# Another order in the last softmax over tokens: the Exp table loaded after the last Sin, a product split in two, exponentials copied first, one copy on VectorE

## The chip, the cores and the metric

The kernel runs on one core of one Trainium2 chip. The metric is the device time of one execution in microseconds (us), the median of several runs. TensorE (PE) multiplies matrices, PEld is its weight load; VectorE (DVE), ScalarE (ACT) and GpSimd (POOL) work on tiles; SyncE (SP) issues the transfers.

## The reference

Three layers in a row. The attention is a recurrence over 768 steps for 4 batches and 8 heads; its output is x, 3072 tokens of 384. Then a wide layer and a soft mixture of experts:

```python
h = x @ w_in                       # 3072 x 2048
x = (h * np.cos(h)) @ w_out        # 3072 x 384
logits = x @ phi                   # 3072 x 32 slots
d = np.exp(logits - logits.max(0, keepdims=True))
d /= d.sum(0, keepdims=True) + 1e-09          # softmax over tokens
slot_input = d.T @ x
...                                # per expert: max(slot_input @ w1[e], 0) @ w2[e]
c = np.exp(logits - logits.max(1, keepdims=True))
c /= c.sum(1, keepdims=True) + 1e-09          # softmax over slots
out = c @ slot_out
```

## The kernel before, in words

Tokens come in 12 groups of 256 (group 0 to 11); the 2048 hidden features come in 8 banks of 256, so a bank is one PSUM tile of 128 x 512. The whole order of the work, for all five engines, is written out by hand in the string HEAD: each word is a step, such as `h.11.4.0` (group 11, bank 4, first half), and each step appends its instructions to the queues of its engines. No scheduler changes it. An engine works its queue strictly in that order; where an instruction needs another engine, it waits on a semaphore, and all behind it wait too.

The steps of a bank, with the lines of the profile:

- `h` (L462 to L464, PE): the product x @ w_in into PSUM, in three passes over 3 x 128 rows.
- `turns` (L474, ACT), `rest` (L478, DVE), `cos` (L482, ACT, a Sin), `mul` (L486, DVE): h is reduced by whole turns, its cosine taken, and g = h cos(h) formed.
- `gT` (L494, PE): g is transposed in four pieces into PSUM; `gc` (L499): the transposed tile is copied to SBUF as gt, on ScalarE, or on VectorE for some banks of the last groups. Of the PSUM tiles that gT of the last groups uses there are two, so a gT waits until an earlier gT's tile has been copied out.
- `l` (L507, PE): g times p = w_out @ phi, the logits of the group, summed over all banks (`l.11.5` takes banks 4 and 5, `l.11.7` banks 6 and 7).

When all banks of a group are done, the softmax over tokens takes a step with a running maximum:

- `sum` (L514) copies the logits l to SBUF as lg, `lc` (L520, PE) adds their four parts into PSUM, `max` (L530 to L535, DVE) updates the running maximum and nb, its negative, and `quart` (L541, ACT) copies the logits, cut into four quarters, into the tile dl.
- `exp`: in groups 0 to 10 the exponential is made from a Silu (L556 on ACT, then L563 to L573 on DVE, steps `xt`, `xr`, `xd`). In group 11 it is a true Exp (L551, and L552 for the factor al). Silu, Sin and the copies run from one ScalarE table, Exp needs another one.
- `dT` (L579, PE) transposes exponentials and logits together into one PSUM tile. `dc` (L586, ACT) copies the exponentials out of it as dt, `ltok` (L592, DVE) copies the logits out of it. Both read the same PSUM bank, and the one that stands second in HEAD waits for the first.
- `E` (L603, PE): dt times the eight tiles gt, first half `E.g.0` with gt 0 to 3, second half `E.g.1` with gt 4 to 7. `es` or `esl` (L612, L614, DVE): e_sb = e_sb al + E.

After group 11 the tail is one chain: slot inputs si (L778), expert products (L797, L837), outputs (L868, L870). The softmax over slots of the last tokens uses an Exp too (L627).

The step `tab` (L699, ACT) is an Exp of one column whose result nobody reads; it stands for its table load. Before the change it is in group 9, between `dc.8` and `turns.9.4`. Two weight tiles of 1.5 MB each are loaded after `h.11.4`, and five more after `E.11.1`.

Of the kernel before, what the change touches and what calls it, by code (L numbers as in the profile page):

```python
# [21 lines left out]
def rwkv_moe_kernel(ctx: ExitStack, tc: tile.TileContext, r, k, v, w, u, w_in, w_out, phi, w1, w2, cst, out):  # L22
    nc = tc.nc
# [13 lines left out]
    NBK = MF // 2  # L37
# [6 lines left out]
    ATT = 77  # L44
# [31 lines left out]
    ltok = const.tile([128, NB, 4, SL], F32, name="ltok")  # L76
# [68 lines left out]
    pend = {}  # L145
# [350 lines left out]

    def b_tc(g, i):
        t = gt_p.tile([128, 2, G], F32, tag="gt", name=f"gt{g}_{i}")
        (nc.vector.tensor_copy if NBK * g + i >= ATT and i in (1, 2) else nc.scalar.copy)(t, pend.pop(("gT", g, i)))  # L499
        gt_t[g, i] = t  # L500

    def b_l(g, i):
# [143 lines left out]
    if True:  # L646
# [51 lines left out]
        def exp_table():  # L698
# [6 lines left out]
                "mask": e_mask, "mc": e_mc, "mp": e_mp, "ksn": e_ksn, "bo": e_bo, "bv": e_bv, "U": e_U, "z": e_z, "rz": e_rz, "st": e_st, "y": e_y, "yb": e_yb,  # L705
                "xh": e_xh, "xl": e_xl, "wn": e_wn, "wc": e_wc,
                "h": b_h, "turns": b_turns, "rest": b_rest, "cos": b_cos, "mul": b_mul, "gT": b_t, "gc": b_tc, "l": b_l,
                "sum": s_sum, "lc": s_logits, "max": s_max, "exp": s_exp, "xt": s_exp_t, "xr": s_exp_r, "xd": s_exp_d, "cmb": s_combine, "we": wide, "att": close_attention, "dT": s_dT, "dc": s_dc, "ltok": s_lc,
                "E": s_e_pe, "es": s_e, "close": close_decode}
# [290 lines left out]
lc.8 mul.9.1 h.9.3.0 ks.23 kN.23 h.9.3.1 yb.21 mask.22 ksn.23 U.23 rest.9.0 y.22 cos.9.0 turns.9.3 rz.23.0 mul.9.0 rest.9.3 ru.23  # L1000
l.9.1 bv.22 yb.22 gT.9.0 cos.9.3 max.8 exp.8 st.23.0 mul.9.3 bo.23 xh.22 gc.9.0 z.23.1 st.23.1 xt.8 xr.8 xd.8 h.9.2.0 h.9.2.1
turns.9.2 rT.23 dT.8 h.9.4.0 xl.22 cmb.1.5 zl.23 rest.9.2 sp.23 cos.9.2 gT.9.1 L.23 gc.9.1 h.9.4.1 gT.8.6 h.9.5.0 h.9.5.1 gc.8.6
xh.21 xl.21 dc.8 tab turns.9.4 cmb.0.5 rest.9.4 turns.9.5 h.9.6.0 gT.9.3 h.9.6.1 rest.9.5 cos.9.5 mul.9.2 A.23 ltok.8 E.8.0 E.8.1
l.9.3 cos.9.4 cmb.2.0 mask.23 bv.23 mul.9.5 gc.9.3 cmb.2.1 rz.23.1 y.23 yb.23 turns.9.6 rest.9.6 xh.23 cos.9.6 h.9.7.0 cmb.2.3
mul.9.6 xl.23 gT.9.2 gc.9.2 mul.9.4 h.9.7.1 turns.9.7 rest.9.7 cos.9.7 mul.9.7 cmb.2.2 gT.9.5 gc.9.5 h.10.0.0 gT.9.4 h.10.0.1
l.9.5 l.9.7 gT.9.6 h.10.2.0 turns.10.0 cmb.2.4 rest.10.0 cos.10.0 mul.10.0 sum.9 es.8 h.10.3.0 h.10.3.1 turns.10.3 rest.10.3
# [6 lines left out]
max.10 exp.10 h.11.2.0 mul.11.0 l.11.1 turns.11.6 gT.11.0 gc.11.0 xt.10 rest.11.6 cos.11.6 h.11.2.1 gc.10.5 turns.11.2 mul.11.6  # L1013
rest.11.2 cos.11.2 mul.11.2 h.11.3.0 h.11.3.1 turns.11.3 rest.11.3 cos.11.3 mul.11.3 gT.10.7 h.11.7.0 h.11.7.1 turns.11.7.0
rest.11.7.0 cos.11.7.0 h.11.5.0 h.11.5.1 l.11.3 turns.11.7.1 gc.10.7 rest.11.7.1 cos.11.7.1 mul.11.7.1 xr.10 gT.11.3 turns.11.5
rest.11.5 cos.11.5 gT.11.2 gc.11.2 xd.10 h.11.4.0 h.11.4.1 turns.11.4 dT.10 mul.11.5 ltok.10 gT.11.6 dc.10 E.10.0 E.10.1 gc.11.3
rest.11.4 cos.11.4 mul.11.4 l.11.5 mul.11.7.0 l.11.7 sum.11 we.6 we.10 gT.11.5 lc.11 gc.11.5 gT.11.4 gc.11.6 max.11 quart.11
exp.11 dT.11 ltok.11 gT.11.7 dc.11 gc.11.4 es.10 gc.11.7 we.7 we.8 E.11.0 esl.11.0 we.9 E.11.1 esl.11.1
"""


# [47 lines left out]
```

## Time and profile before

| | |
|---|---|
| median of 3 runs | 549.68 us (548.1 to 550.96) |
| the profiled execution | 549.77 us, of which its span (first to last instruction) 548.0 us |
| mean granted TensorE clock | 0.981 |
| busy in the span | PE 503.2 us, PEld 435.7, DVE 433.4, ACT 315.5, POOL 125.3 |
| chain that ended last | PE 62%, DVE 21%, ACT 8%, DMA 4%, issue 3% |

Matmuls are pipelined, so a row's duration overlaps with the next; what an engine waits for is read from the idle time before a row, given in brackets, and from the distance between starts. A clock of 1.00 is 2.4 GHz, 0.50 is 1.2 GHz. Times in the rows below are counted from the start of the span.

### The profile page before, as it was taken

What the parts mean: (1) busy time and instruction counts of PE and PEld (TensorE: products, weight loads), DVE (VectorE), ACT (ScalarE), POOL (GpSimd) and SP (SyncE); (2) the same over time, 40 slices, a digit from 0 to 9 for tenths busy, and PEclk for the clock granted to TensorE, in tenths of its full rate; (3) what the DMA queues carried; (4) which work ended last, traced back from release to release, by engine and by line L of the source; (5) the groups of instructions that cost most, each with busy time, mean ns of one, the idle gap of its engine ahead of it and who ended that gap; (6) DMA issues with size and microseconds to landing.
All of it is one profiled execution on the core that took longest, in us unless ns stands there. A gap on an engine that the chain in (4) does not pass through costs nothing.

```text
span 548.0 us, 16247 instructions
## 1 busy us (share of the span) xinstructions
PE 503.2 (92%) x6850; PEld 435.7 (80%) x6850; DVE 433.4 (79%) x823; ACT 315.5 (58%) x661; POOL 125.3 (23%) x163
## 2 busy tenths in 40 slices
PE   2777879989999999999999999999999999997994
PEld 1546667879898898998988988999888899883674
DVE  4999898998889879887878898989788867664423
ACT  3256567646757465666555754656557756664422
POOL 4520120254044213321420420533034000000400
PEclk9988999999999999999999999999999999998997
DMA  8994656444432433411440342173031683377949
GB/s 209 268 240 110 157 115 182 123 75 74 74 60 44 76 57 60 74 35 27 75 73 10 66 89 45 22 132 54 16 60 32 232 317 144 112 264 275 403 175 273
DMA packets 146712, 67.52 MB, mean 123 GB/s; under 512 B 127568, under 2 KB 134736, under 8 KB 146640
## 3 DMA queue, kind: packets, MB, share of 16 engines
q1 hardware_dynamic: 146640, 66.49, 47.9%
q8 instruction: 54, 0.88, 0.7%
q14 instruction: 18, 0.15, 0.1%
HBM read 61.75 MB, written 4.72 MB: 121 GB/s over the span
## 4 chain that ended last, share of the span: by engine, by line
PE 62%; DVE 21%; ACT 8%; DMA 4%; issue 3%; SPq 0%; ACTq 0%; DVEq 0%
PE h L462 9%; PE h L464 9%; PE h L463 9%; PE gT L494 6%; PE E L603 4%; PE l L507 3%; DMA rawi<-in_moe_w_in_dram 3%; PE y L288 3%; PE A L208 3%; DVE L L222 2%; PE U L259 2%; DVE g L478 2%; PE hps L797 2%; PE so L837 2%; DVE pt L164 2%
## 5 line engine op out<-in xcount | busy, mean ns | idle before, releaser
L462 PE MATMUL h<-x,wu 128*128 128x256 f32 x573 | 172.0, 300 | 1.3 <-DVE g L486 1.3
L464 PE MATMUL h<-x,wu 128*128 128x256 f32 x573 | 161.4, 282 | 1.2 <-ACT wu L410 1.2
L463 PE MATMUL h<-x,wu 128*128 128x256 f32 x573 | 161.3, 281 | 0.0
L462 PEld LDWEIGHTS h<-x,wu 128*128 128x128 f32 x573 | 109.2, 191 | 3.5 <-DVE g L486 1.7
L464 PEld LDWEIGHTS h<-x,wu 128*128 128x128 f32 x573 | 109.0, 190 | 1.4 <-ACT wu L410 1.4
L463 PEld LDWEIGHTS h<-x,wu 128*128 128x128 f32 x573 | 109.3, 191 | 0.2
L482 ACT ACTIVATE g<-g,half_pi 128x512 f32<-128x512 f32 (+1 forms) x97 | 69.4, 719 | 42.4 <-DVE g L478 41.4
L486 DVE TENSOR_TENSOR g<-g,h 128x512 f32<-128x512 f32 x96 | 64.8, 677 | 28.0 <-ACT g L482 27.5
L474 ACT ACTIVATE g<-h 128x512 int32<-128x512 f32 x96 | 57.0, 596 | 39.8 <-PE h L464 32.9
L478 DVE SCALAR_TENSOR_TENSOR g<-g,h 128x512 f32<-128x512 int32 x96 | 65.0, 678 | 16.8 <-ACT g L474 15.7
L251 POOL TENSOR_TENSOR bv<-vz,bo 64x384 f32<-64x384 f32 x48 | 43.9, 914 | 140.1 <-DVE bo L243 78.1
L499 ACT COPY gt<-gT 128x512 f32<-128x512 f32 x92 | 53.3, 583 | 31.2 <-PE gT L494 30.6
L494 PE MATMUL gT<-cs,g 128*128 128x128 f32 x384 | 58.1, 275 | 0.3 <-ACT gt L499 0.2
L494 PEld LDWEIGHTS gT<-cs,g 128*128 128x128 f32 x384 | 43.7, 140 | 6.2 <-issue 3.3
L169 POOL TENSOR_TENSOR ru<-rn,u_b 128x384 f32<-128x384 f32 x24 | 27.3, 1136 | 58.2 <-issue 19.5
L193 POOL MEMSET L<- 64x512 f32 x32 | 16.7, 521 | 96.1 <-PE y L288 81.5
L156 DVE TENSOR_TENSOR_SCAN qt<-wf,one_b 128x520 f32<-128x520 f32 x24 | 30.5, 1270 | 7.3 <-ACT wf L151 7.2
L222 DVE TENSOR_TENSOR L<-A,cs 64x512 f32<-64x512 f32 x48 | 33.1, 689 | 3.8 <-PE A L208 2.6
L274 ACT COPY rzs<-z 64x192 f32<-64x192 f32 x96 | 33.4, 348 | 3.6 <-DVE z L269 2.6
L187 DVE TENSOR_TENSOR L<-rT,pt 64x512 f32<-64x512 f32 x48 | 32.9, 686 | 1.6 <-PE rT L141 0.6
L164 DVE TENSOR_TENSOR_SCAN pt<-wf,ini_f 128x520 f32<-128x520 f32 x24 | 31.7, 1320 | 0.1
L208 PE MATMUL A<-L,ks 128*64 128x64 f32 (+1 forms) x768 | 28.1, 226 | 2.8 <-DVE ks L199 2.1
(175 smaller groups left out, 836.3 us busy)
## 6 DMA issues: line engine op xcount, KB each, us to landing
we<-in_moe_w_dram SPq DMA_DIRECT2D x16, 1536.0 KB, 10.4
rawi<-in_moe_w_in_dram SPq DMA_DIRECT2D x7, 768.0 KB, 6.0
wn<-in_w_dram SPq DMA_DIRECT2D x24, 192.0 KB, 4.1
kn<-in_k_dram SPq DMA_DIRECT2D x24, 192.0 KB, 3.9
rn<-in_r_dram SPq DMA_DIRECT2D x24, 192.0 KB, 3.9
vz<-in_v_dram SPq DMA_DIRECT2D x48, 96.0 KB, 3.2
rzs<-in_v_dram SPq DMA_DIRECT2D x96, 48.0 KB, 2.8
out_dram<-ob SPq DMA_DIRECT2D x17, 256.0 KB, 3.7
```

The source lines that it names most:

```text
L208: nc.tensor.matmul(ps[64 - 64 * a:128 - 64 * a, s, :], lhsT=ks[k, s, :], rhs=L[k, a, s, :], start=True, stop=True)
L222: nc.vector.tensor_tensor(out=L[h, a], in0=ps[h], in1=mask[h].unsqueeze(1).to_broadcast([64, NS, C]), op=ALU.mult)
L251: nc.gpsimd.tensor_tensor(out=bv[h], in0=vn_t[j][h, :, c, :], in1=bo[h].to_broadcast([64, H, D]), op=ALU.mult)
L462: nc.tensor.matmul(hp, lhsT=wh, rhs=xh[:, c, :], start=(c == 0), stop=False)
L463: nc.tensor.matmul(hp, lhsT=wh, rhs=xl[:, c, :], start=False, stop=False)
L464: nc.tensor.matmul(hp, lhsT=wl, rhs=xh[:, c, :], start=False, stop=(c == KD - 1))
L474: nc.scalar.activation(gt.bitcast(I32), hp, AF.Copy, bias=0.25, scale=1.0 / TWO_PI)
L478: nc.vector.scalar_tensor_tensor(out=gt, in0=gt.bitcast(I32), scalar=-TWO_PI, in1=hp, op0=ALU.mult, op1=ALU.add)
L482: nc.scalar.activation(gt, gt, AF.Sin, bias=half_pi[:, 0:1])
L486: nc.vector.tensor_tensor(out=gt, in0=gt, in1=hp, op=ALU.mult)
L494: nc.tensor.transpose(ps[:, tt, mm, :], gt[:, mm, tt * 128:(tt + 1) * 128], ident)
L499: (nc.vector.tensor_copy if NBK * g + i >= ATT and i in (1, 2) else nc.scalar.copy)(t, pend.pop(("gT", g, i)))
```

## The change

Five things are done, four of them by moving words in HEAD:

1. `tab` leaves group 9 and stands behind `cos.11.4`, the last Sin of the kernel.
2. `rest.11.4` and `cos.11.4` move ahead of the copies that stood before them (`ltok.10` on DVE, `gc.11.3` on ACT); `gc.11.3` now stands behind `tab`.
3. `E.10.1` leaves its place behind `E.10.0` and stands behind `lc.11`; so do `es.10` and `gc.11.5`, later than `max.11`.
4. In groups 10 and 11 `dc` stands ahead of `ltok`.
5. `gc` of bank 5 runs on VectorE in groups 9, 10 and 11, where it ran on ScalarE.

```diff
-        (nc.vector.tensor_copy if NBK * g + i >= ATT and i in (1, 2) else nc.scalar.copy)(t, pend.pop(("gT", g, i)))
+        (nc.vector.tensor_copy if NBK * g + i >= ATT and i in (1, 2, 5) else nc.scalar.copy)(t, pend.pop(("gT", g, i)))
...
-xh.21 xl.21 dc.8 tab turns.9.4 cmb.0.5 rest.9.4 turns.9.5 h.9.6.0 gT.9.3 h.9.6.1 rest.9.5 cos.9.5 mul.9.2 A.23 ltok.8 E.8.0 E.8.1
+xh.21 xl.21 dc.8 turns.9.4 cmb.0.5 rest.9.4 turns.9.5 h.9.6.0 gT.9.3 h.9.6.1 rest.9.5 cos.9.5 mul.9.2 A.23 ltok.8 E.8.0 E.8.1
...
-rest.11.5 cos.11.5 gT.11.2 gc.11.2 xd.10 h.11.4.0 h.11.4.1 turns.11.4 dT.10 mul.11.5 ltok.10 gT.11.6 dc.10 E.10.0 E.10.1 gc.11.3
-rest.11.4 cos.11.4 mul.11.4 l.11.5 mul.11.7.0 l.11.7 sum.11 we.6 we.10 gT.11.5 lc.11 gc.11.5 gT.11.4 gc.11.6 max.11 quart.11
-exp.11 dT.11 ltok.11 gT.11.7 dc.11 gc.11.4 es.10 gc.11.7 we.7 we.8 E.11.0 esl.11.0 we.9 E.11.1 esl.11.1
+rest.11.5 cos.11.5 gT.11.2 gc.11.2 xd.10 h.11.4.0 h.11.4.1 turns.11.4 dT.10 mul.11.5 rest.11.4 gT.11.6 dc.10 cos.11.4 tab ltok.10
+E.10.0 mul.11.4 l.11.5 mul.11.7.0 l.11.7 sum.11 gc.11.3 gT.11.5 gc.11.6 lc.11 we.6 we.10 E.10.1 max.11 quart.11 exp.11 gc.11.5
+gT.11.4 es.10 dT.11 gT.11.7 dc.11 ltok.11 gc.11.4 gc.11.7 we.7 we.8 E.11.0 esl.11.0 we.9 E.11.1 esl.11.1
```

ScalarE's queue in the last group, before, from dc.10 to dc.11 (gt_3 is the copy gc.11.3, g_4 the cosine cos.11.4, dl the quarters and then the exponentials, dt the copied exponentials):

```order
L586 COPY dt_7319<-dT_7309 64x64 x2
L499 COPY gt_3_7339<-gT_3_7270 128x512
L482 ACTIVATE g_4_7307<-g_4_7307,half_pi 128x512
L499 COPY gt_5_7366<-gT_5_7359 128x512
L499 COPY gt_6_7373<-gT_6_7314 128x512
L541 COPY dl_112<-lc_7364 32x64 x4
L551 ACT_TABLE_LOAD
L551 ACTIVATE dl_112,sg_7385<-dl_112,nb_7378 128x64
L552 ACTIVATE al_7384<-dl_112,nb_7378 128x1
L586 COPY dt_7397<-dT_7388 64x64 x2
```

The same piece of ScalarE's queue in the changed kernel:

```order
L586 COPY dt_7317<-dT_7308 64x64 x2
L482 ACTIVATE g_4_7306<-g_4_7306,half_pi 128x512
L699 ACT_TABLE_LOAD
L699 ACTIVATE half_pi<-half_pi 128x1
L499 COPY gt_3_7345<-gT_3_7269 128x512
L499 COPY gt_6_7352<-gT_6_7312 128x512
L541 COPY dl_112<-lc_7354 32x64 x4
L551 ACTIVATE dl_112,sg_7378<-dl_112,nb_7371 128x64
L552 ACTIVATE al_7377<-dl_112,nb_7371 128x1
L586 COPY dt_7397<-dT_7390 64x64 x2
```

The table load moved from just before the Exp to just behind the last Sin; gc.11.3 went behind it, and gc.11.5 left the queue.

TensorE's queue in the same place, before, from the last product of group 10 to the transpose of the exponentials:

```order
L603 MATMUL E_7322<-gt_7_7264,dt_7319 32x256
L507 MATMUL l_7152<-g_4_7307,p_sb 32x256 x2
L507 MATMUL l_7152<-g_5_7275,p_sb 32x256 x2
L507 MATMUL l_7152<-g_6_7157,p_sb 32x256 x2
L507 MATMUL l_7152<-g_7_7236,p_sb 32x256 x2
L494 MATMUL gT_5_7359<-cs,g_5_7275 128x128 x4
L520 MATMUL lc_7364<-lg_7353,cs 128x256
L494 MATMUL gT_4_7368<-cs,g_4_7307 128x128 x4
L579 MATMUL dT_7388<-cs,dl_112 128x128
```

And in the changed kernel, from the last product of E.10.0 to the first of E.10.1:

```order
L603 MATMUL E_7324<-gt_3_6988,dt_7317 32x256
L507 MATMUL l_7151<-g_4_7306,p_sb 32x256 x2
L507 MATMUL l_7151<-g_5_7274,p_sb 32x256 x2
L507 MATMUL l_7151<-g_6_7156,p_sb 32x256 x2
L507 MATMUL l_7151<-g_7_7235,p_sb 32x256 x2
L494 MATMUL gT_5_7347<-cs,g_5_7274 128x128 x4
L520 MATMUL lc_7354<-lg_7343,cs 128x256
L603 MATMUL E_7324<-gt_4_7057,dt_7317 32x256
```

The eight products of E.10.1 moved behind lc.11; the transposes gT.11.4 and dT.11 follow them.

VectorE's queue before, from mul.11.5 to lg (the copy of `sum`):

```order
L486 TENSOR_TENSOR g_5_7275<-g_5_7275,h_5_7240 128x512
L592 COPY ltok<-dT_7309 64x2x32 x2
L478 SCALAR_TENSOR_TENSOR g_4_7307<-g_4_7307,h_4_7288 128x512
L486 TENSOR_TENSOR g_4_7307<-g_4_7307,h_4_7288 128x512
L486 TENSOR_TENSOR g_7_7236<-g_7_7236,h_7_7216 128x256
L514 COPY lg_7353<-l_7152 128x256
```

And in the changed kernel:

```order
L486 TENSOR_TENSOR g_5_7274<-g_5_7274,h_5_7239 128x512
L478 SCALAR_TENSOR_TENSOR g_4_7306<-g_4_7306,h_4_7287 128x512
L592 COPY ltok<-dT_7308 64x2x32 x2
L486 TENSOR_TENSOR g_4_7306<-g_4_7306,h_4_7287 128x512
L486 TENSOR_TENSOR g_7_7235<-g_7_7235,h_7_7215 128x256
L514 COPY lg_7343<-l_7151 128x256
```

rest.11.4 changed places with ltok.10.

## Rows read from the trace of the kernel before

**Rows 1.** Timeline of TensorE, last group: start us, us, engine, line, operation [idle before].
```profile
490.14 0.27 PE L579 MATMUL dT<-cs,dl 128*128 128x128 f32 x1
...
491.67 1.93 PE L603 MATMUL E<-gt,dt 128*32 128x256 f32 x32 [0.82 <-ACT dt L586]
493.63 1.07 PE L507 MATMUL l<-g,p_sb 128*32 128x256 f32 x16
494.63 0.66 PE L494 MATMUL gT<-cs,g 128*128 128x128 f32 x4
495.24 0.70 PE L520 MATMUL lc<-lg,cs 128*128 128x256 f32 x2
...
499.10 0.33 PE L579 MATMUL dT<-cs,dl 128*128 128x128 f32 x1 [2.48 <-ACT dl L551]
...
500.49 3.33 PE L603 MATMUL E<-gt,dt 128*32 128x256 f32 x32 [0.63 <-ACT dt L586]
...
504.94 2.81 PE L778 MATMUL si<-wo_sb,et 128*32 128x256 f32 x64
```

**Rows 2.** Timeline of ScalarE in the same stretch.
```profile
490.34 0.60 ACT L474 ACTIVATE g<-h 128x512 int32<-128x512 f32 x1 [0.43 <-PE h L464]
491.20 0.42 ACT L586 COPY dt<-dT 64x64 f32<-64x64 f32 x2 [0.26 <-DVE ltok L592]
491.65 0.59 ACT L499 COPY gt<-gT 128x512 f32<-128x512 f32 x1
492.13 0.72 ACT L482 ACTIVATE g<-g,half_pi 128x512 f32<-128x512 f32 x1
...
496.44 0.85 ACT L541 COPY dl<-lc 32x64 f32<-32x64 f32 x4
497.31 1.28 ACT L551 ACT_TABLE_LOAD   x1
498.60 0.35 ACT L551 ACTIVATE dl<-dl,nb 128x64 f32<-128x64 f32 x1
...
500.02 0.42 ACT L586 COPY dt<-dT 64x64 f32<-64x64 f32 x2 [0.79 <-DVE ltok L592]
```

**Rows 3.** Timeline of VectorE in the same stretch.
```profile
491.14 0.69 DVE L478 SCALAR_TENSOR_TENSOR g<-g,h 128x512 f32<-128x512 int32 x1
492.88 1.02 DVE L486 TENSOR_TENSOR g<-g,h 128x512 f32<-128x512 f32 x2 [1.05 <-ACT g L482]
494.76 0.42 DVE L514 COPY lg<-l 128x256 f32<-128x256 f32 x1 [0.86 <-PE l L507]
495.98 0.42 DVE L530 TENSOR_REDUCE mx<-lc 128x1 f32<-128x256 f32 x1 [0.79 <-PE lc L520]
...
499.46 0.47 DVE L592 COPY ltok<-dT 64x64 f32<-64x64 f32 x2 [2.67 <-PE dT L579]
```

**Rows 4.** Windows: stretch, length, busy PE, PEld, DVE, ACT, POOL, granted clock, DMA, GB/s.
```profile
500.00:502.00 2.00, 1.51 (x16) 0.80 (x20) 0.84 (x2) 1.48 (x4) 0.82 (x1) 0.50 0.03 11
```

**Rows 5.** Timeline of ScalarE and of TensorE's weight load around the old tab, group 9.
```profile
430.53 1.28 ACT L699 ACT_TABLE_LOAD   x1
431.82 0.20 ACT L699 ACTIVATE half_pi<-half_pi 128x1 f32<-128x1 f32 x1
...
438.18 0.64 PEld L288 LDWEIGHTS y<-L,rzs 128*32 128x32 f32 x32 [0.46 <-ACT rzs L274]
```

**Rows 6.** All waits of TensorE from 425 to 492 us: total us, times, longest.
```profile
PE E L603 <- ACT dt L586: 0.8, 1, 0.8
PE y L288 <- ACT rzs L274: 0.3, 1, 0.3
```

**Rows 7.** Timeline of VectorE where the copies of bank 5 come in, groups 9 to 11.
```profile
450.55 0.69 DVE L478 SCALAR_TENSOR_TENSOR g<-g,h 128x512 f32<-128x512 int32 x1 [0.84 <-ACT g L474]
...
475.19 0.68 DVE L499 COPY gt<-gT 128x512 f32<-128x512 f32 x1
...
480.29 0.69 DVE L486 TENSOR_TENSOR g<-g,h 128x512 f32<-128x512 f32 x1 [1.49 <-ACT g L482]
```

## The prediction

> **What bounds the kernel now.** I read the page first: TensorE has most of the chain that ended last, so before asking what an edit saves I ask whether TensorE waits there. The list of its waits answers that for the whole stretch from group 9 to the end of h.11.4: two entries in 67 us, one of 0.3 us and one of 0.8 [rows 6]. So up to dT.10 (490.14) TensorE is the bound, and work taken from ScalarE there gains only what TensorE stood waiting for. From 490.14 on it is different. The three timelines of the last group [rows 1 to 3], read together from row to row, show one dependent chain through three engines with TensorE mostly idle: turns.11.4 490.34, rest 491.14, cos 492.13, mul 492.88, l 493.63, the copy lg 494.76, lc 495.24, max 495.98, quart 496.44, table load 497.31, Exp 498.60, dT.11 499.10, ltok 499.46, dc.11 500.02, E.11 500.49, which ends at 503.82. All that follows hangs on that end: the slot inputs start behind it [rows 1], and the five late weight loads are issued after it, so they shift with it. Last the windows: at 500 to 502 the granted clock is 0.50, 1.2 GHz [rows 4]. E.11 takes 3.33 us for the 32 rows that took E.10 1.93 [rows 1]. What TensorE did before the fall was to wait 2.48 us for the Exp, and then only transposes [rows 1].
>
> **The change part by part.** All sums are against the profiled execution, 549.77 us, 0.09 above the median of the runs shown.
>
> *The old tab.* It removes three table loads from ScalarE, for its own Exp and for the Sin and the Silu that had to load back (one of the three stands in the rows), and a 0.20 us activation: 3 x 1.28 + 0.20 = 4.04 us of ScalarE [rows 5]. TensorE saw of it only its wait for the last copy rz.23, 0.46 us by the weight load's row [rows 5], 0.3 by the list of waits [rows 6]. The ends are 0 and 0.46. I take 0.46, since behind it TensorE has no other wait up to E.10, and E.10's wait lies behind h.11.4.
>
> *The copies of bank 5 on VectorE.* Each is 0.68 us there [rows 7] and leaves ScalarE 0.59 us [rows 2]. In group 9 the copy goes ahead of work that a little later leaves VectorE idle for 0.84 us; in group 10 it falls into an idle 1.49 us [rows 7]. Both are covered, though the first with little to spare; uncovered, each could cost up to 0.68. In group 11 it stands behind max.11, where VectorE had nothing to do until ltok at 499.46, idle 2.67 us [rows 3]; only gT.11.7 waits for it. I take 0 for all three. es.10 goes into the same idle time.
>
> *rest and cos forward.* turns.11.4 ends at 490.94 [rows 2]; rest can start at 490.98 instead of 491.14. It ends 0.69 later, 491.67. cos, which no longer waits for gc.11.3, starts at 491.70 instead of 492.13: 0.43 saved. mul and l follow at the old distances, 492.45 and 493.20 [rows 1, 3], and lg at 494.33. dc.10 no longer waits for ltok.10 [rows 2], so it follows turns.11.4 at about 490.85 and E.10.0 starts near 491.3; half of E.10's 1.93 is done by 492.3, before l needs TensorE.
>
> *The new place of tab, and a wait that it adds.* cos ends at 492.42; load 1.28, activation 0.20, gc.11.3 0.59: the copy ends at 494.49. gT.11.5 needs the PSUM tile that this copy frees, and lc stands behind gT.11.5 on TensorE. So gT.11.5 starts at about 494.52, only 0.11 before its old 494.63 [rows 1]. If lc keeps its old distance of 0.61 to it, 0.11 is saved; if lc hangs on lg alone, as before, 0.43. I take 0.3, as the old 0.61 was set by lg (494.76 + 0.42), not by the transposes: lc at 494.94.
>
> *Exp without its load.* quart starts 1.20 behind lc in the old trace, when max (495.98 + 0.42) and ScalarE's two copies end together [rows 2, 3]. max alone gives the same distance: quart at 496.14. The Exp comes 0.87 behind it, where the load started: 497.01 against 498.60, 1.59 saved; dT.11 at 497.51.
>
> *dc ahead of ltok.* dc.11 starts 0.92 behind dT.11 now, because ltok reads the bank first; ltok starts 0.36 behind it [rows 1 to 3]. With places changed dc.11 starts at 497.87 and E.11 0.47 later, 498.34, against 500.49: 2.15 saved. E.11.1 needs gc.11.4 and gc.11.7, which stay behind dc on ScalarE: 2 x 0.59 from 498.29, ready by 499.5. Its product with gt 7 comes at about 499.5, so I count nothing for it, at most 0.2.
>
> *E.11 at full clock.* Between lc and dT.11 TensorE now has E.10.1 (half of 1.93) and gT.11.4, so the wait of 2.48 shrinks to below 0.7. I take the clock to stay at 2.4 GHz. E.11 then takes 1.93 instead of 3.33 [rows 1], 1.40 saved. The ends for this term are 0 and 1.40.
>
> Sum: 0.46 + 2.15 + 1.40 = 4.0 us off. 549.77 - 4.0 = **545.8 us**.
>
> The load's price is where rule and rows part. In the trace the load takes 1.28 us, starts 0.02 after the last quarter copy and is followed by the Exp within 0.01 [rows 2]; the load of group 9 likewise is followed at once [rows 5]. The Trainium skill, "ScalarE: Activation LUTs", section "What ACT_TABLE_LOAD costs", gives about 1283 ns for the load and about 1380 ns more for a drain, 2.66 us for each switch. By that figure gc.11.3 would end 1.38 us later, and by an estimate from it the sum would be about 2.6 us instead of 4.0. The rows show the 1283 ns and no drain, so I go by them.
>
> **The rivals.**
>
> *A. The clock still falls before E.11.* For it: E.10.0 leaves a new gap before l (E.10.0 ends near 492.3, l starts at 493.20), and from E.10.1 to E.11 there are again transposes only, about 2 us. Against it: the gap of 0.82 before E.10 left E.10 at 1.93 [rows 1], and the long idle is gone. E.11 keeps its 3.33: 549.77 - 0.46 - 2.15 = 547.2.
>
> *B. The early gain is lost on VectorE.* For it: gc.9.5 stands in VectorE's queue ahead of a rest and a mul whose PSUM tile a later h needs, and the idle time behind it is only 0.84 [rows 7]. If it delays TensorE by its 0.68 and the 0.46 don't arrive: 549.77 - 4.0 + 0.46 + 0.68 = 546.9.
>
> *C. The load holds gc.11.3 longer.* If a switch behind a running Sin costs one load's length more, 1.28, then gT.11.5, lc and all behind come 1.28 later: 547.1. Against it: each load in the rows runs on without a gap. The drain of that page of the Trainium skill is such a mechanism, with nearly this price.
>
> *D. Slower.* The mechanism is the same clock at another place: it falls in the new gap before l.11.5 and stays at 1.2 GHz until the slot inputs are done. By E.11's ratio 3.33/1.93 = 1.73 [rows 1], l gains 0.78, lc 0.5, E.11 1.40 over the forecast and si 2.05: 4.7 in all, against 4.0 saved, so 550.5, and more if it lasts into the expert products. It decides from about 8 us at the low clock on. Against it: the mean granted clock of the whole span is 0.981, and TensorE has more to do in this stretch than before, not less.
>
> That the change doesn't do what it says I exclude: the queues show one load left behind the first, and none before the Exp.
>
> **How the numbers follow.** Forecast 0.66, A 0.16, B 0.11, C 0.04, D 0.03. 0.5% is 2.75 us, about what a measurement of this kernel can tell from no change; it puts the border at 546.9. The forecast lies 1.1 below it and A, C just above; B is on it. Faster: 0.61 of the forecast, half of B and 0.05 of A: 0.72. Slower by more than 0.5%: 0.02 of D. The rest, 0.26, is within. The range: down to 544.7, with the runs of before spread over 2.86 us and lc at its better end; up to 547.6, which takes in A, B and C with a little for that spread.
>
> **What would show it.** In the changed profile: one table load besides the first, right behind the last Sin; no wait of y for rz.23; gT.11.5 waiting for gc.11.3; Exp within 0.1 us of quart's end; dc.11 about 0.36 behind dT.11 and ltok behind it; E.11 starting about 2.6 earlier and lasting about 1.9 at clock 1.00; the stretch from E.11's end to the end of the span unchanged. I am wrong if E.11 still shows 0.50, if a PE wait on a rest or mul appears in groups 9 to 11, or if the tail behind E.11 lengthens, for instance because a weight load comes late.

## The result

| | before | changed |
|---|---|---|
| median of 5 runs each | 549.68 us (548.1 to 550.96) | 544.25 us (542.96 to 545.2) |
| ratio | | 0.9909, 95% interval 0.9886 to 0.9931 |
| the profiled execution | 549.77 us, span 548.0 | 544.25 us, span 542.5 |
| mean granted clock | 0.981 | 0.98 |

The changed kernel is faster by 0.9%. It lies on the side that was forecast, but 1.55 us below the forecast of 545.8 and 0.45 below the low end of the range, 544.7.

### The profile after

The timeline of TensorE in the changed kernel, last group (start us, us, engine, line, operation, idle before it), which answers to [rows 1]:

```profile
488.02 0.27 PE L579 MATMUL dT<-cs,dl 128*128 128x128 f32 x1
488.13 0.60 PE L494 MATMUL gT<-cs,g 128*128 128x128 f32 x4
490.18 1.07 PE L603 MATMUL E<-gt,dt 128*32 128x256 f32 x16 [1.46 <-DVE ltok L592]
491.06 1.07 PE L507 MATMUL l<-g,p_sb 128*32 128x256 f32 x16
492.33 0.66 PE L494 MATMUL gT<-cs,g 128*128 128x128 f32 x4 [0.20 <-ACT gt L499]
492.82 0.60 PE L520 MATMUL lc<-lg,cs 128*128 128x256 f32 x2
493.35 1.07 PE L603 MATMUL E<-gt,dt 128*32 128x256 f32 x16
494.35 0.66 PE L494 MATMUL gT<-cs,g 128*128 128x128 f32 x4
495.30 0.33 PE L579 MATMUL dT<-cs,dl 128*128 128x128 f32 x1 [0.28 <-ACT dl L551]
495.46 0.60 PE L494 MATMUL gT<-cs,g 128*128 128x128 f32 x4
496.13 2.15 PE L603 MATMUL E<-gt,dt 128*32 128x256 f32 x32
...
499.38 2.81 PE L778 MATMUL si<-wo_sb,et 128*32 128x256 f32 x64
```

The wait of 2.48 us ahead of dT.11 has become 0.28, and E.11 takes 2.15 us instead of 3.33. There is a wait that nobody forecast, 1.46 us ahead of E.10.0.

ScalarE in the same stretch, which answers to [rows 2]:

```profile
488.71 0.41 ACT L586 COPY dt<-dT 64x64 f32<-64x64 f32 x2
489.57 0.72 ACT L482 ACTIVATE g<-g,half_pi 128x512 f32<-128x512 f32 x1 [0.45 <-DVE g L478]
490.31 1.28 ACT L699 ACT_TABLE_LOAD   x1
491.60 0.20 ACT L699 ACTIVATE half_pi<-half_pi 128x1 f32<-128x1 f32 x1
491.71 1.06 ACT L499 COPY gt<-gT 128x512 f32<-128x512 f32 x2
493.92 0.85 ACT L541 COPY dl<-lc 32x64 f32<-32x64 f32 x4 [1.15 <-DVE mx L530]
494.80 0.35 ACT L551 ACTIVATE dl<-dl,nb 128x64 f32<-128x64 f32 x1
...
495.66 0.42 ACT L586 COPY dt<-dT 64x64 f32<-64x64 f32 x2 [0.23 <-PE dT L579]
496.11 1.07 ACT L499 COPY gt<-gT 128x512 f32<-128x512 f32 x2
```

The load now stands right behind the last Sin, and the Exp follows the quarter copies at once. The copies between them run without a further load. dc.11 waits for dT.11 alone.

VectorE there, which answers to [rows 3], and ahead of it the copy of bank 5 in group 9, which answers to the first of [rows 7]:

```profile
443.65 0.68 DVE L499 COPY gt<-gT 128x512 f32<-128x512 f32 x1
...
448.42 0.69 DVE L478 SCALAR_TENSOR_TENSOR g<-g,h 128x512 f32<-128x512 int32 x1 [0.24 <-ACT g L474]
...
488.85 0.69 DVE L478 SCALAR_TENSOR_TENSOR g<-g,h 128x512 f32<-128x512 int32 x1 [0.34 <-ACT g L474]
489.57 0.47 DVE L592 COPY ltok<-dT 64x64 f32<-64x64 f32 x2
490.32 1.02 DVE L486 TENSOR_TENSOR g<-g,h 128x512 f32<-128x512 f32 x2 [0.29 <-ACT g L482]
492.20 0.42 DVE L514 COPY lg<-l 128x256 f32<-128x256 f32 x1 [0.86 <-PE l L507]
493.46 0.42 DVE L530 TENSOR_REDUCE mx<-lc 128x1 f32<-128x256 f32 x1 [0.83 <-PE lc L520]
```

The copy of group 9 was taken out of idle time, 0.84 us before and 0.24 now; in group 10 the 1.49 us of [rows 7] became 0.88.

The granted clock over E.11 in the windows (columns as in [rows 4], which had 0.50 there), and y of group 9 on TensorE, which was broken by the wait of [rows 5] and is now one run of 64 products; TensorE waits nowhere from 425 to 487 us, where [rows 6] had two waits up to 492:

```profile
496.00:498.00 2.00, 1.93 (x33) 1.04 (x32) 1.07 (x4) 1.16 (x3) 0.82 (x1) 1.00 0.90 350
```
```profile
433.60 1.93 PE L603 MATMUL E<-gt,dt 128*32 128x256 f32 x32
435.79 1.08 PE L288 MATMUL y<-L,rzs 128*32 128x64 f32 x64
436.79 0.55 PE L297 MATMUL y<-cs,bv 128*128 128x128 f32 x3
```

### The profile page after: what moved, and what is told of

Same layout as the page of the kernel before. It is cut to its first block, busy times and chain, and to the rows that moved or that the text cites. A ratio compares the mean times of both kernels' runs of the same rounds, so it can differ in the third digit from the quotient of the medians.

```text
span 542.5 us, 16245 instructions
## 1 busy us (share of the span) xinstructions
PE 502.9 (93%) x6850; PEld 436.4 (80%) x6850; DVE 435.2 (80%) x826; ACT 310.7 (57%) x655; POOL 125.4 (23%) x163
## 4 chain that ended last, share of the span: by engine, by line
PE 67%; DVE 18%; ACT 5%; DMA 4%; issue 2%; SPq 2%; DVEq 0%; ACTq 0%
PE h L462 10%; PE h L464 10%; PE h L463 10%; PE gT L494 6%; PE l L507 4%; PE E L603 3%; PE A L208 3%; PE y L288 3%; PE U L259 2%; DMA vz<-in_v_dram 2%; PE hps L797 2%; DMA rawi<-in_moe_w_in_dram 2%; PE so L837 2%; DVE L L222 2%; DVE pt L164 2%
## 5 line engine op out<-in xcount | busy, mean ns | idle before, releaser
L499 ACT COPY gt<-gT 128x512 f32<-128x512 f32 x89 | 51.6, 584 | 28.7 <-PE gT L494 28.1
L156 DVE TENSOR_TENSOR_SCAN qt<-wf,one_b 128x520 f32<-128x520 f32 x24 | 30.6, 1275 | 7.3 <-ACT wf L151 7.3
```

The source lines that it names most:

```text
L499: (nc.vector.tensor_copy if NBK * g + i >= ATT and i in (1, 2, 5) else nc.scalar.copy)(t, pend.pop(("gT", g, i)))
```

## Where the 5.5 us between the two profiles lie

The two spans differ by 5.5 us, but 1.3 of it is there before anything that the change touches. My marker is a scan of the attention on VectorE (L156), on code that is the same in both kernels. It is the 23rd of 24 such scans in either kernel; the expectations below call it the last, which it is not. It starts at these times, first in the kernel before, then in the changed one:

```profile
394.20 1.24 DVE L156 TENSOR_TENSOR_SCAN qt<-wf,one_b 128x520 f32<-128x520 f32 x1
```
```profile
392.87 1.24 DVE L156 TENSOR_TENSOR_SCAN qt<-wf,one_b 128x520 f32<-128x520 f32 x1
```

So I cut each profile into three: the **head** up to the start of this scan, the **middle** from there to the start of si, which holds all of the change, and the **tail** from si to the end of the span. Head, middle and tail are 394.20, 110.74 and 43.06 us before, and 392.87, 106.51 and 43.12 after. The middle lost 4.23 us.

Theory T: the change is worth what the middle shows, and the head scatters from execution to execution. Rival R: the changed kernel has a shorter head each time. Inside the middle most parts of the change were tested for their own price; the cosine's new place ahead of gc.11.3 was not undone by itself. The diffs below show only the words of HEAD that move. Each expectation counts from the start of the scan either to the end of the span or, in the last three, to the start of si; both readings stand in the table. I go by the start of si, because the tails turned out to scatter too, from 42.88 to 43.26 us.

| run | head | middle | middle against the changed kernel | scan to end of span | TensorE's wait at dT.11 | length of E.11 |
|---|---|---|---|---|---|---|
| before | 394.20 | 110.74 | +4.23 | 153.80 | 2.48 | 3.33 |
| e1, before again | 392.16 | 110.70 | +4.19 | 153.74 | 2.48 | 3.30 |
| e2 | 391.60 | 109.61 | +3.10 | 152.6 | 2.48 | 2.72 |
| changed | 392.87 | 106.51 | 0 | 149.63 | 0.28 | 2.15 |
| e8, changed again | 394.14 | 106.50 | -0.01 | 149.76 | 0.28 | 2.15 |
| e3 | 392.96 | 107.79 | +1.28 | 150.94 | 1.56 | 2.15 |
| e4 | 392.64 | 107.38 | +0.87 | 150.26 | 1.44 | 2.15 |
| e5 | 390.87 | 107.13 | +0.62 | 150.03 | 0.28 | 2.15 |
| e6 | 391.28 | 106.83 | +0.32 | 149.82 | 0.28 | 1.93 |
| e7 | 393.07 | 106.42 | -0.09 | 149.63 | none | 1.93 |
| e9 | 392.46 | 106.30 | -0.21 | 149.24 | 0.28 | 1.93 |
| e11 | 390.39 | 109.68 | +3.17 | 152.81 | 2.71 | 2.71 |
| e12 | 392.72 | 106.70 | +0.19 | 149.68 | 0.28 | 2.15 |

Two profiles of one kernel agree in the middle to 0.04 us, while heads lie anywhere from 390.39 to 394.20. The scans of L156 show where the heads part: in the 13 traces the first of them, at about 6 us, starts within 0.8 us, the seventh, at about 115 us, within 3.5, and the marker within 3.8. So nearly all of the scatter arises in the first 115 us.

## The experiments

### Is the head a matter of the kernel? (e1, e8)

Both kernels were run again without an edit.

> The kernel before, unchanged, so that its first 394 us are seen a second time. Theory T: those 394 us are the same code in both kernels and their length scatters from execution to execution by 1 to 2 us, so the start of the last scan over tokens (L156) can fall anywhere from 392 to 395 us here, while the stretch from that start to the end of the span stays at 153.8 us within 0.3. Rival R: the kernel before reaches that scan late each time, at 394.2 us within 0.3, and the changed one early, at 392.9.

> The changed kernel, unchanged, so that its first 393 us are seen a second time. Theory T: from the start of the last scan to the end 149.63 us within 0.3, while that start itself may fall anywhere from 392 to 395 us. Rival R: it falls at 392.9 us within 0.3 again.

Measured: 547.82 us (545.49 to 549.32) for the kernel before, 544.22 (542.53 to 545.65) for the changed one. The heads changed places: 392.16 before, 394.14 after. R falls, and T stands, though its 392 was too high: four other heads lie between 390.39 and 391.60. The marker in the two repeats, that of the kernel before first:

```profile
392.16 1.24 DVE L156 TENSOR_TENSOR_SCAN qt<-wf,one_b 128x520 f32<-128x520 f32 x1
```
```profile
394.14 1.24 DVE L156 TENSOR_TENSOR_SCAN qt<-wf,one_b 128x520 f32<-128x520 f32 x1
```

Over all 68 runs of the kernel before, on several chips, the median is 548.52 us and the mean 548.38 (545.04 to 551.14); 10 of them are at 549.68 or above. The 11 runs of the changed kernel have a mean of 544.14. The means differ by 4.24 us, the middle by 4.2.

### The old table load alone (e2)

```diff
-dc.8 tab turns.9.4
+dc.8 turns.9.4
```

> The kernel before with one edit: the table load ahead of group 9's turns is taken out, so that the load comes back ahead of the last Exp, as before. Measured from the start of the last scan to the end of the span. Theory T: the 0.78 us that the changed kernel had gained at E.8 and y of group 9 is due to this load alone, so 153.1 us (153.80 less 0.7 to 0.8), and the engine time of y is one unbroken run of 64. Rival: the 0.78 us comes from another order of the queues and the load is worth the 0.46 us of its own wait at most, 153.3 to 153.4.

Measured: 547.29 us, ratio to the kernel before 0.9973 (0.9956 to 0.999); the middle 1.1 us shorter. To the end it takes 152.6, which is 0.5 below T. From the scan to dT.10 it takes 95.22 us, against 95.94 before and 95.15 in the changed kernel: 0.72 of the 0.79 us is this load, nearly as T has it, and more than the 0.46 of the rival. In the kernel before y of group 9 begins, breaks and goes on like this:

```profile
437.23 0.65 PE L288 MATMUL y<-L,rzs 128*32 128x64 f32 x32
438.19 0.80 PE L288 MATMUL y<-L,rzs 128*32 128x64 f32 x32 [0.30 <-ACT rzs L274]
438.92 0.55 PE L297 MATMUL y<-cs,bv 128*128 128x128 f32 x3
```

From the first product to the next line's it is 1.69 us here and 1.00 in the unbroken row of the changed kernel: the break costs 0.69, more than either wait that is named for it. The remaining 0.4 us of e2 are not the load: after the same 2.48 us of waiting the granted clock was low already under dT.11 and came back earlier in E.11. E.11 started 1.54 us behind dT.11, where it had been 1.39 in the kernel before, but took 2.72 us and not 3.33:

```profile
495.78 0.48 PE L579 MATMUL dT<-cs,dl 128*128 128x128 f32 x1 [2.48 <-ACT dl L551]
...
497.32 2.72 PE L603 MATMUL E<-gt,dt 128*32 128x256 f32 x32 [0.21 <-ACT dt L586]
```

### Parts of the new order undone (e3 to e6)

e3, no early load:

```diff
-cos.11.4 tab ltok.10
+cos.11.4 ltok.10
```

> The changed kernel without its early table load: everything else of its order stays, and the load falls ahead of the last Exp again (1.28 us on ScalarE). Measured from the start of the last scan to the end, the changed kernel has 149.63 us. Theory T: the Exp comes 1.28 us later less the little that ScalarE waited ahead of it, so TensorE waits at dT.11 for 1.3 to 1.4 us where it waited 0.28, the clock stays at 2.4 GHz over E.11 since the wait is shorter than the 2.48 us of before, and the stretch is 150.7 us. Rival, the clock: the wait is enough for the granted clock to fall over E.11, which then takes 3.3 us as before, and the stretch is 152.0 to 152.2 us.

Measured: 545.73 us, ratio 0.9945 (0.9927 to 0.9963). The load is back ahead of the Exp, and TensorE waits at dT.11 for exactly its length more, 1.56 against 0.28:

```profile
494.87 1.28 ACT L551 ACT_TABLE_LOAD   x1
496.17 0.35 ACT L551 ACTIVATE dl<-dl,nb 128x64 f32<-128x64 f32 x1
```
```profile
496.66 0.33 PE L579 MATMUL dT<-cs,dl 128*128 128x128 f32 x1 [1.56 <-ACT dl L551]
...
497.50 2.15 PE L603 MATMUL E<-gt,dt 128*32 128x256 f32 x32
```

The clock stayed at 1.00, so T holds and its rival falls: the load by itself is worth 1.28 us.

e4, E.10 in one piece:

```diff
-E.10.0 mul.11.4 l.11.5
+E.10.0 E.10.1 mul.11.4 l.11.5
...
-we.10 E.10.1 max.11
+we.10 max.11
```

> The changed kernel with the second half of E of group 10 put back behind the first. Theory T: the 16 products (1.07 us) then stand ahead of l.11.5, lg and lc, and the max, Exp and dT.11 come 0.9 to 1.0 us later, TensorE waits at dT.11 for 1.2 to 1.3 us more than now; from the start of the last scan to the end 150.6 us against 149.63. Rival, the clock: the longer wait at dT.11 lets the granted clock fall, E.11 takes 3.3 us, and the stretch is 152 us. Rival, no matter: the split is hidden, because the softmax waits for its scores (mul, lg) on VectorE and not for TensorE, and the stretch is 149.6 us.

Measured: 544.76 us, ratio 0.9924 (0.9907 to 0.9941), middle +0.87. The split is not hidden; T's price was nearly right, and the clock held through a wait of 1.44 us:

```profile
490.04 1.93 PE L603 MATMUL E<-gt,dt 128*32 128x256 f32 x32 [1.46 <-DVE ltok L592]
...
493.37 0.70 PE L520 MATMUL lc<-lg,cs 128*128 128x256 f32 x2
...
495.94 0.33 PE L579 MATMUL dT<-cs,dl 128*128 128x128 f32 x1 [1.44 <-ACT dl L551]
```

The 0.87 is a price within the new order. E.10 starts 2.17 us behind dT.10 here and started 1.53 behind it in the kernel before; lc comes 5.50 behind dT.10 and came 5.10. So the split in part only makes good the later start of E.10 that the other moves bring.

e5, the copies of dT.11 in the old order:

```diff
-gT.11.7 dc.11 ltok.11
+gT.11.7 ltok.11 dc.11
```

> The changed kernel with the copies of dT.11 in the old order: VectorE's transposed turns (ltok) ahead of ScalarE's copy of the exponentials (dc). Both read the one bank that dT.11 fills. Theory T: ScalarE's copy waits for VectorE's, as it did before (0.79 us ahead of dc.11 in rows of the kernel before, 0.23 in the changed one), E.11 starts 0.5 to 0.6 us later, and the stretch from the start of the last scan to the end is 150.2 us against 149.63. Rival: the two engines read the bank side by side and the order is worth nothing, 149.6 us.

Measured: 544.1 us, ratio 0.9917 (0.9895 to 0.9938), middle +0.62. ScalarE's copy waits 0.81 us for VectorE's, against 0.23 in the changed kernel, and E.11 behind it:

```profile
494.28 0.42 ACT L586 COPY dt<-dT 64x64 f32<-64x64 f32 x2 [0.81 <-DVE ltok L592]
```
```profile
494.75 2.15 PE L603 MATMUL E<-gt,dt 128*32 128x256 f32 x32 [0.66 <-ACT dt L586]
```

e6, bank 5 back on ScalarE:

```diff
-i in (1, 2, 5) else
+i in (1, 2) else
```

> The changed kernel with the copies of bank 5 (gc.9.5, gc.10.5, gc.11.5) back on ScalarE. Theory T: those of groups 9 and 10 cost nothing on either engine, since TensorE waits for neither; gc.11.5 now stands between the last Exp and dc.11 on ScalarE and takes about 0.6 us there, of which TensorE's transposes hide a part, so E.11 starts about 0.3 us later: 149.9 us against 149.63 from the start of the last scan. Rival: the copies on VectorE had held up its own turns in groups 9 and 10, and taking them back gains there what is lost in group 11: 149.6 us or less.

Measured: 543.84 us, ratio 0.9919 (0.9897 to 0.9941), middle +0.32. From the scan to dT.10 it is 95.14 us, with the copies on VectorE 95.15: in groups 9 and 10 the move costs and gains nothing. All of the 0.32 arises in group 11, where gc.11.5 stands between the Exp and dc.11, and gT.11.7 waits for it:

```profile
494.48 0.66 PE L494 MATMUL gT<-cs,g 128*128 128x128 f32 x4 [0.47 <-ACT gt L499]
```

The runs' medians could not have told these last prices from nothing: e6 is 0.3 us longer in its middle and has a lower median than the changed kernel. The cut profile does. The prices of e2 to e6 (0.72, 1.28, 0.87, 0.62, 0.32) need not add up to the 4.23 of the middle: each was measured beside the other parts, and the clock's share, below, is in none of them.

### Does the clock depend on that wait? (e11)

e3 and e4 together.

> The changed kernel with two parts undone at once: no early table load (e3) and the second half of E of group 10 back behind the first (e4). Each alone cost 1.28 and 0.87 us from the start of the last scan to the start of si and left the granted clock at 1.00. Theory T: the wait of TensorE ahead of dT.11 grows to 2.4 us (1.56 in e3 plus 0.9), which is as long as in the kernel before, so the granted clock falls to 0.50 (1.2 GHz) and E.11 takes 2.7 to 3.3 us: 106.51 + 1.28 + 0.87 + 0.6 to 1.2, that is 109.3 to 109.9 us. Rival: the clock fell in the kernel before for another reason (the wait ahead of E.11, or an earlier idle time), it stays at 1.00 here and the two prices only add: 108.65 us.

Measured: 546.72 us, ratio to the kernel before 0.9973 (0.9956 to 0.9989), middle +3.17, where the two prices add up to 2.15. The wait is 2.71 us, and behind it the granted clock is low:

```profile
494.98 0.47 PE L579 MATMUL dT<-cs,dl 128*128 128x128 f32 x1 [2.71 <-ACT dl L551]
495.25 1.06 PE L494 MATMUL gT<-cs,g 128*128 128x128 f32 x4
496.24 2.71 PE L603 MATMUL E<-gt,dt 128*32 128x256 f32 x32
```
```profile
494.00:496.00 2.00, 1.02 (x5) 0.93 (x5) 0.11 (x2) 1.57 (x7) 0.00 (x0) 0.61 0.71 275
496.00:498.00 2.00, 2.00 (x22) 0.88 (x24) 0.39 (x2) 1.01 (x2) 0.82 (x1) 0.53 0.00 0
```

T holds: the clock cost 3.17 - 2.15 = 1.0 us here. After waits of 0.28, 1.44 and 1.56 us at this place the clock stayed at 1.00, after 2.48 and 2.71 it fell. So with the rest of the change in place either the load's new place or the split is enough to hold the clock, and only without both is it lost.

### The unforeseen wait (e12)

```diff
-mul.11.5 rest.11.4 gT.11.6 dc.10 cos.11.4 tab ltok.10
+mul.11.5 ltok.10 gT.11.6 dc.10 rest.11.4 cos.11.4 tab
```

> The changed kernel with ltok.10 back ahead of rest.11.4 on VectorE, and dc.10 ahead of cos.11.4 as it is. In the changed kernel TensorE waits 1.46 us at E.10.0, for ltok.10, since E of group 10 is written into the bank that ltok.10 still reads. Theory T: that wait costs nothing, because the products behind E.10.0 (l.11.5) need mul.11.4, which ends about when E.10.0 does; so E.10.0 starts 0.5 to 0.8 us earlier and gains nothing, and rest.11.4 and the cosine come 0.1 to 0.2 us later: 106.6 to 106.7 us from the start of the last scan to the start of si against 106.51. Rival: the wait was a cost, and without it l, lc and the softmax come up to 0.5 us earlier: 106.0 to 106.3 us.

Measured: 543.4 us, ratio 0.9905 (0.9887 to 0.9923), middle +0.19. E.10.0 now starts early, and TensorE simply waits behind it instead, for mul:

```profile
489.42 1.07 PE L603 MATMUL E<-gt,dt 128*32 128x256 f32 x16 [0.82 <-ACT dt L586]
491.11 1.07 PE L507 MATMUL l<-g,p_sb 128*32 128x256 f32 x16 [0.62 <-DVE g L486]
```

l starts 3.22 us behind dT.10 here and 3.04 in the changed kernel. The 1.46 us are free: the longest wait of the stretch is not on the path.

### A version that beats both? (e7, e9)

e7 moves two copies that the changed kernel's rows show to be late: gc.11.3, for which gT.11.5 waits 0.20 us, and gc.11.7, for whose copy the product of E.11 with gt 7, the 20th of 32, waits.

```diff
-rest.11.5 cos.11.5 gT.11.2
+rest.11.5 gc.11.3 cos.11.5 gT.11.2
...
-gT.11.4 es.10 dT.11 gT.11.7 dc.11 ltok.11 gc.11.4 gc.11.7 we.7
+gT.11.4 es.10 gT.11.7 gc.11.7 dT.11 dc.11 ltok.11 gc.11.4 we.7
```

with gc.11.7 on VectorE (`or (g, i) == LAST`).

> A version meant to be faster than the changed kernel: gc.11.3 is moved ahead of the cosine of 11.5 on ScalarE, and the last transposes of group 11 (gT.11.7) with their copy are put ahead of dT.11, the copy on VectorE. Theory T: in the changed kernel lc started late because gc.11.3 stood behind the table load (TensorE waited 0.20 us ahead of gT.11.5), and the last product of E.11 waited for gc.11.7 (E.11 took 2.15 us for 32 products, against 1.07 for 16 that wait for nothing); with both out of the way the stretch from the start of the last scan to the end is 149.3 us against 149.63. Rival: gT.11.7 ahead of dT.11 takes 0.6 us of TensorE where it only idled for 0.28, and the cosines come later by gc.11.3's 0.6 us, so nothing is gained or up to 0.3 us lost: 149.6 to 149.9 us.

Measured: 543.97 us, ratio 0.9913 (0.9893 to 0.9934), middle -0.09: E.11 is back to 1.93 us, but dT.11 comes 7.42 us behind dT.10, not 7.28. So its place behind gT.11.7 took most of the gain, as the rival said; to the end of the span it is 149.63, the changed kernel's time. e9 puts dT.11 first again:

```diff
-es.10 gT.11.7 gc.11.7 dT.11 dc.11 ltok.11 gc.11.4 we.7
+es.10 dT.11 gT.11.7 dc.11 gc.11.7 ltok.11 gc.11.4 we.7
```

> e7 with its last transposes (gT.11.7) back behind dT.11; gc.11.3 stays early and gc.11.7 stays on VectorE, now behind dc.11 and ahead of ltok.11. Measured from the start of the last scan to the start of si, where the changed kernel has 106.51 and 106.50 us in its two profiles and e7 106.42. Theory T: in e7 dT.11 started 0.18 us later than the exponentials allowed because gT.11.7 stood ahead of it; without that both gains count, E.11 is 1.93 us long and starts after dc.11, 106.25 us. Rival: dT.11's 0.18 us is a wait that e7 only showed elsewhere, 106.4 us.

Measured: 543.94 us, ratio 0.9914 (0.9896 to 0.9932), middle -0.21, with dT.11 7.23 us behind dT.10; at 106.30 against a forecast of 106.25, T holds. In the profile it beats both kernels; its median differs from the changed kernel's 544.22 by less than the runs scatter.

## Why the prediction was right and wrong

Distances from dT.10, before and after, with what was forecast:

| step | before | after | saved | forecast |
|---|---|---|---|---|
| scan to dT.10 (old tab) | 95.94 | 95.15 | 0.79 | 0.46 |
| rest.11.4 | 1.00 | 0.83 | 0.17 | 0.16 |
| cos.11.4 | 1.99 | 1.55 | 0.44 | 0.43 |
| lc.11 | 5.10 | 4.80 | 0.30 | 0.30 |
| Exp | 8.46 | 6.78 | 1.68 | 1.59 |
| start of E.11 | 10.35 | 8.11 | 2.24 | 2.15 |
| length of E.11 | 3.33 | 2.15 | 1.18 | 1.40 |
| sum of the first and the last two | | | 4.21 | 4.01 |

**The mechanism was right, and its sum nearly.** The chain from turns.11.4 to E.11 went as the part on it said, and the clock stayed up. gT.11.5 waited for gc.11.3 behind the load, and lc started 0.13 us later than the cosine's 0.43 would have allowed. That lc saved just the 0.30 forecast is partly luck, as the figure was a choice between 0.11 and 0.43; and lc then took 0.60 us in place of 0.70, so max and quart came 0.40 earlier and not 0.30, which accounts for the 0.09 by which the Exp and E.11 beat their forecast. "TensorE mostly idle" was too strong: from dT.10 to E.11 its rows show 3.9 idle us in 10.35 [rows 1]; no term rests on it. The load ran on without a gap: 490.31 load, 491.60 dummy, 491.71 gc.11.3, and e3 prices it at its own 1.28 us. The further 1.38 us that the Trainium skill, "ScalarE: Activation LUTs", section "What ACT_TABLE_LOAD costs", gives for a drain shows in no run here. None of the rivals came true: the clock was 1.00 over l, lc and E.11 (A and D), the stretch up to dT.10 gained rather than lost (B), and gc.11.3 was not held (C). In rival D the break-even of "about 8 us at the low clock" fits a loss of half of that time; by the ratio of 1.73 that D itself uses it is 9.5.

**The step that failed is the base, and the room that the range left for it.** All sums start from one execution, 549.77 us, which the median of three runs, 549.68, seemed to confirm, and the low end of 544.7 allows that base only about 1 us. The head of that execution, 394.20 us, is the longest of 13 profiled ones, which lie within 3.8 us, and 549.68 is a high draw: the mean of all runs of that kernel is 548.38. From there the forecast's own 4.0 us give 544.4, and the 4.2 of the middle 544.2; 544.25 was measured. Nothing slowed that whole set of runs: the five of the changed kernel taken with it average 544.17, the six of e8 544.11. The three runs on the table went down to 548.1, and a range that allowed this as the base would have reached 544.1. That the head is what made the unprofiled runs long is argued from the profiles and not shown.

**Two terms were mis-sized, in opposite directions.** That the sum is only 0.2 us off is thus partly luck. The old tab was put at 0.46, the weight load's wait; it brought 0.72 alone and 0.79 in the changed kernel. Its upper end, 0.46, was no bound: the broken y also lost the overlap of its two halves. The distance between the starts of y and of the line behind it, 1.69 us, set against 1.00 for an unbroken y, would have shown it. E.11 was put at 1.93 with "at most 0.2" for the product with gt 7; that product did wait for gc.11.7, E.11 is 0.22 us longer for it, and e6, e7 and e9 show 1.93 where the copy is early enough.

**One wait was overlooked.** E.10.0 was put at 491.3 in the old trace's time, 1.16 us behind dT.10; it came 2.16 behind, because E of group 10 is written into the bank that ltok.10 still reads, and ltok.10 had moved behind rest.11.4. It cost nothing by the chance that mul is later still (e12).

Of the copies on VectorE the 0 for groups 9 and 10 was right (e6). In group 11 the move is worth 0.32, because there it leaves ScalarE free between the Exp and dc.11.

## What to carry to other kernels

Before a forecast is set against one profiled time, cut the span at a marker ahead of the change and ask how the part in front of it scatters; here two profiles of one kernel agree to 0.04 us in the part that holds the change and differ by 2 us ahead of it, so a cut profile prices edits of 0.2 us that no median of a few runs can show, as long as the clock does the same in both profiles. Price a broken instruction stream by the distance between starts, not by the wait that is named for it. Where two edits shorten the same idle time, the clock that falls behind it is one gain and not two: it is kept by either and counted once.

## What was not expected of the hardware

The granted clock did not fall at the same place behind the same wait. In the kernel before and in e1 it fell behind dT.11's 2.48 us only shortly before E.11 (0.93 from 497 to 498 us in e1, 0.50 in the next three); in e2, behind the same 2.48 us, dT.11 itself already ran slowly, 0.48 us instead of 0.33, and E.11 got part of its clock back, which made it 0.6 us shorter. An experiment that leaves such a wait in place can thus read 0.4 us off, as e2 did. Why the heads differ by up to 3.8 us was not tried and stays open; the traces show only that they part in the first 115 us.
